# Reordering attention work inside a tuned linear-attention + MLP kernel: kv between transposes, num beside den, and a copy of v on ScalarE

## The chip, the cores and the metric

The kernel runs on one core of a Trainium2 chip. The metric is the device time of one execution in microseconds (us), as a median of several runs; the profile's span is some 1.7 us shorter than the time of the same run (294.94 against 293.2).

## The reference

```python
# q, k, v: (8 batches, 8 heads, 576 positions, 64), float32
def phi(x): return np.where(x > 0, x, np.exp(x) - 1.0) + 1.0
q_p, k_p = phi(q), phi(k)
kv  = einsum('bhsd,bhse->bhde', k_p, v)
z   = sum(k_p, axis=2)
num = einsum('bhsd,bhde->bhse', q_p, kv)
den = einsum('bhsd,bhd->bhs', q_p, z)[..., None] + 1e-06
x   = (num / den), heads side by side: (4608 tokens, 512)
h   = x @ w_in                # 512 -> 2048
out = (h - np.tanh(h)) @ w_out  # 2048 -> 512
```

## The kernel before

The two dense layers run over nine chunks of 512 tokens. Layer 1 makes 16 pieces of hidden features per chunk (4 matmuls each), layer 2 has 16 steps of 4 matmuls. The attention of the later batches is cut into small parts that are hung behind single pieces (`s1[piece]`) or steps (`s2[step]`). In these traces each engine does its work in program order, so the place of a part decides what stands ahead of it on every engine that it uses. In the names, phi, kv, num and den are those of the reference, kz is kv after the mask, and PSUM (`ps_all` in the lines) is the memory, in banks, in which the matmuls' results arrive.

```python
# attention parts (cut)
def a_qT_pe(b, i, banks, on=None):      # 9 TensorE transposes of q's phi, copied out by ScalarE and VectorE
    ...
def a_kv(b, banks):                     # 36 matmuls phi(k)^T v, then the mask product by VectorE -> kz
    ...
def a_vp(b, i):                         # v with its two heads side by side, by VectorE
    nc.vector.tensor_copy(vp[:, i, :, 0:128].rearrange(...), v_b[b % 2][:, 0:2, i])
def a_kv_cols(b, banks):                # the same kv from vp: 36 matmuls, then VectorE's mask products
    ...
    for hg in range(2):
        nc.vector.tensor_mul(kz_t[b][:, hg, :, 0:136], ps[hg], mask[:, hg, :, 0:136])
def a_den(b, banks):                    # 16 small matmuls with kz, then add and reciprocal by VectorE
    ...
def a_spread(b):                        # reciprocals to DRAM (ds) and back, copied to all partitions (rdb)
    ...
def a_num(b, p):                        # one num matmul, then xT = num * rdb by VectorE; two PSUM banks
    ...
# piece pair of layer 1 (cut): tanh by ScalarE, then the subtraction by VectorE
def l1act2(fi, h, gT):
    th = mpool.tile([128, 2, 512], F32, name="th")
    nc.scalar.activation(th, h, AF.Tanh)
    nc.vector.tensor_sub(gT[:, fi:fi + 2, :], h, th)

# chunk 0 (cut)
s2[7].append(lambda: (a_qT_pe(1, 0, side), a_qT_pe(1, 1, side), a_kv(1, side)))
s2[8].append(lambda: b0_scale_rest(side))
s2[9].append(lambda: a_den(1, side))
s2[10].append(lambda: (num1(), a_split(1)))     # num of batch 1: 8 matmuls, five copies (ns) by ScalarE
s2[11].append(lambda: spread1(0))               # reciprocals spread by TensorE, scale by VectorE
# chunk 1 (cut): n1 = 2, n2 = 3
s1[7 if c == 1 else 5].append(lambda: a_kv_cols(n1, attn))
s1[10 if c == 1 else 8].append(lambda: (a_den(n1, attn), a_spread(n1)))
for p in range(NP + 1):
    s2[(11 if c == 1 else 9) + p].append(lambda p=p: a_num(n1, p))
# (cut)
s1[0].append(lambda: (gate(qT_t[n1]), load_k(n2), load_q(n2), load_v(n2)))
#   gate: GpSimd copies one element of q's transpose, so the loads wait for that transfer
```

## Time and profile before

| | before |
|---|---|
| median time | 294.82 us (three runs, 294.65 to 294.93) |
| TensorE busy | 285.2 us of 293.2 (97%) |
| VectorE, ScalarE busy | 60%, 48% |
| gaps of TensorE in the stretch that the change touches | about 2.0 us in all |

The columns of a timeline are: start, length, engine, line, operation, output and inputs, number of instructions merged, and in brackets the idle time of the engine just before with what ended it. A matmul's start is exact, its end is modelled, and starts 0.216 us apart are TensorE's full pace here; so I compare starts. TensorE's lines up to den are shown in the prediction. These are TensorE's later ones, then VectorE's queue ahead of kz (line L202), then the transfers of the reciprocals of batch 2 by SyncE (ds to DRAM, rdb back, here broadcast to all partitions):

```profile
67.30 10.52 PE L387 MATMUL ps_all<-w_out_sb,gT 128*128 128x512 bf16 x48
...
79.85 0.38 PE L317 MATMUL ps_all<-qT,kz 128*128 128x512 bf16 x1
...
58.97 2.34 DVE L373 TENSOR_TENSOR gT<-ps_all,th 128x1024 bf16<-128x1024 f32 x2
61.23 0.78 DVE L202 TENSOR_TENSOR kz<-ps_all,mask 128x272 bf16<-128x272 f32 x2
...
65.45 1.29 SPq L305 DMA_DIRECT2D ds<-rden  x4
70.65 1.12 SPq L308 DMA_DIRECT2D rdb<-ds  x2
```

### The profile page before, as it was taken

To read this page: it belongs to the slowest core of one execution; us is meant where nothing else is said; L and a number is where in the kernel's file an instruction comes from. 1 tells how busy PE (TensorE), PEld (TensorE's weight loads), DVE (VectorE), ACT (ScalarE), POOL (GpSimd) and SP (SyncE) were. 2 spreads that over 40 slices of the span, in tenths; PEclk is the share of its full clock that TensorE was granted. 3 is DMA by queue.
4 is the path that set the end of the run, shared out by engine and by line. 5 is a ranking of instruction groups with operands and counts; after the bars stand their busy time and mean duration, and the time that the engine had idled before them with its cause. 6 is when DMAs were issued, how large, how long until landed. Compare 5 with 4: busy or idle time off the path is not lost.

```text
span 293.2 us, 4504 instructions
## 1 busy us (share of the span) xinstructions
PE 285.2 (97%) x1801; PEld 134.3 (46%) x1801; DVE 174.6 (60%) x265; ACT 139.6 (48%) x168; POOL 33.3 (11%) x55
## 2 busy tenths in 40 slices
PE   8899999999999999999999999999999999999994
PEld 2544453454444444444444445444444444444443
DVE  4759857887567764786478646865581456106600
ACT  4938536947344643455246524661552155126411
POOL 8673030030030003000300020000000000000000
PEclk9999999999999999999999999999999999999999
DMA  6999999998999758955895669667117310131032
GB/s 101 194 204 212 208 207 216 200 145 153 234 163 185 160 118 139 218 117 129 136 223 127 139 134 183 134 154 143 38 24 178 73 36 0 38 84 24 0 74 72
DMA packets 39077, 38.94 MB, mean 133 GB/s; under 512 B 16336, under 2 KB 33808, under 8 KB 38288
## 3 DMA queue, kind: packets, MB, share of 16 engines
q0 software_dynamic: 17552, 18.35, 38.6%
q1 hardware_dynamic: 21344, 20.17, 30.3%
q8 instruction: 14, 0.23, 0.3%
q10 hardware_dynamic: 160, 0.13, 0.1%
q14 instruction: 7, 0.06, 0.1%
HBM read 43.91 MB, written 9.55 MB: 182 GB/s over the span
## 4 chain that ended last, share of the span: by engine, by line
PE 79%; DMA 11%; issue 7%; POOL 2%; DVE 0%; ACT 0%; POOLq 0%
PE ps_all L387 37%; PE ps_all L366 36%; DMA qraw<-in_q_dram 6%; DMA w_in_sb<-in_moe_w_in_dram 3%; PE ps_all L199 2%; DMA kraw<-in_k_dram 2%; PE ps_all L317 2%; PE ps_all L604 1%; PE ps_all L276 1%; POOL qraw L90 0%; ACT e L134 0%; POOL kraw L93 0%; DVE qp L136 0%; POOL v L93 0%; POOL w_out_sb L115 0%
## 5 line engine op out<-in xcount | busy, mean ns | idle before, releaser
L366 PE MATMUL ps_all<-xT,w_in_sb 128*128 128x512 bf16 x576 | 128.0, 379 | 0.3 <-DVE xT L244 0.3
L387 PE MATMUL ps_all<-w_out_sb,gT 128*128 128x512 bf16 x560 | 127.8, 379 | 0.0
L373 DVE TENSOR_TENSOR gT<-ps_all,th 128x1024 bf16<-128x1024 f32 x64 | 77.9, 1218 | 59.8 <-ACT th L372 59.8
L372 ACT ACTIVATE th<-ps_all 128x1024 f32<-128x1024 f32 x64 | 65.5, 1024 | 57.0 <-PE ps_all L366 47.1
L366 PEld LDWEIGHTS <-w_in_sb 128*128 128x128 bf16 x576 | 55.3, 98 | 66.6 <-issue 0.6
L387 PEld LDWEIGHTS <-gT 128*128 128x128 bf16 x560 | 54.1, 98 | 64.3 <-issue 0.3
L396 ACT COPY osb<-ps_all 128x512 f32<-128x512 f32 (+1 forms) x36 | 20.9, 583 | 73.4 <-PE ps_all L387 54.2
L328 DVE TENSOR_TENSOR xT<-ps_all,rdb 128x512 bf16<-128x512 f32 x24 | 16.3, 689 | 13.4 <-PE ps_all L317 11.2
L134 ACT ACTIVATE e<-qraw 128x1152 bf16<-128x1152 bf16 x16 | 18.5, 1162 | 6.9 <-DMA qraw<-in_q_dram 6.9
L134 ACT ACTIVATE e<-kraw 128x1152 bf16<-128x1152 bf16 x15 | 17.5, 1166 | 0.2 <-DMA kraw<-in_k_dram 0.2
L136 DVE TENSOR_TENSOR qp<-e,r 128x1152 bf16<-128x1152 bf16 x16 | 12.0, 757 | 7.8 <-ACT e L134 7.2
L136 DVE TENSOR_TENSOR kp<-e,r 128x1152 bf16<-128x1152 bf16 x15 | 11.4, 759 | 8.3 <-ACT e L134 7.5
L383 POOL COPY g<-qT 1x1 bf16<-1x1 bf16 x5 | 1.2, 240 | 120.6 <-DMA qT<-qp 120.6
L378 DVE TENSOR_TENSOR gT<-ps_all,th 128x512 bf16<-128x512 f32 x16 | 10.3, 685 | 2.4 <-ACT th L377 1.7
L377 ACT ACTIVATE th<-ps_all 128x512 f32<-128x512 f32 x16 | 9.2, 598 | 4.3 <-PE ps_all L366 3.1
L317 PE MATMUL ps_all<-qT,kz 128*128 128x512 bf16 x28 | 10.1, 379 | 0.0
L444 PE MATMUL ps_all<-zero 128*128 128x512 bf16 x29 | 8.8, 463 | 1.2 <-DVE zero L405 1.2
L135 DVE TENSOR_SCALAR r<-qraw 128x1152 bf16<-128x1152 bf16 x16 | 7.3, 453 | 2.2 <-DMA qraw<-in_q_dram 2.2
L199 PE MATMUL ps_all<-vp,kp 64*128 64x136 bf16 x216 | 7.4, 220 | 0.4 <-POOL g L383 0.4
L199 PEld LDWEIGHTS <-kp 64*128 64x128 bf16 x216 | 6.4, 94 | 3.0 <-issue 2.1
L285 DVE RECIPROCAL rden<-den 128x144 f32<-128x144 f32 x7 | 7.4, 1053 | 0.2
L394 DVE COPY osb<-ps_all 128x128 f32<-128x128 f32 x1 | 0.3, 292 | 11.6 <-PE ps_all L604 11.6
(82 smaller groups left out, 121.7 us busy)
## 6 DMA issues: line engine op xcount, KB each, us to landing
out_dram<-osb SPq DMA_DIRECT2D x70, 128.0 KB
rdb<-ds SPq DMA_DIRECT2D x12, 576.0 KB
kraw<-in_k_dram POOLq DMA_DIRECT2D x7, 576.0 KB, 7.1
qraw<-in_q_dram POOLq DMA_DIRECT2D x7, 576.0 KB, 9.0
v<-in_v_dram POOLq DMA_DIRECT2D x7, 576.0 KB, 12.2
w_out_sb<-in_moe_w_out_dram POOLq DMA_DIRECT2D x4, 512.0 KB, 16.4
w_in_sb<-in_moe_w_in_dram POOLq DMA_DIRECT2D x6, 256.0 KB, 8.6
qraw<-in_q_dram POOLq DMA_DIRECT2D x2, 288.0 KB, 4.6
```

The source lines that it names most:

```text
L134: return (lambda: nc.scalar.activation(e, x, AF.Exp), lambda: nc.vector.tensor_scalar(r, x, 0.0, 1.0, ALU.max, ALU.add), lambda: nc.vector ...
L136: lambda: nc.vector.tensor_tensor(y, e, r, ALU.min))
L199: nc.tensor.matmul(ps[hg][:, i, :], kp[r, i, j].rearrange("p h d -> p (h d)"), vp[r, i, j, :], start=(j == 0), stop=(j == J - 1))
L317: nc.tensor.matmul(ps, kz[:, p // 2, p % 2, 0:128], qT[:, p % 2, 0:8, p // 2, :], start=True, stop=True)
L328: nc.vector.tensor_mul(xT[:, p, S * b:S * b + 512].rearrange("p (j t c) -> p j t c", j=8, t=4), ps.rearrange("p j (t c) -> p j t c", t=4), ...
L366: nc.tensor.matmul(h, w_in_sb[:, 2 * (p % 2) + p // 2, fi * 128:(fi + 1) * 128], xT[:, p, c * 512:(c + 1) * 512], start=(n == 0), stop=(n ...
L372: nc.scalar.activation(th, h, AF.Tanh)
L373: nc.vector.tensor_sub(gT[:, fi:fi + 2, :], h, th)
L377: nc.scalar.activation(th, h, AF.Tanh)
L378: nc.vector.tensor_sub(gT[:, fi, :], h, th)
L387: nc.tensor.matmul(o, gT[:, fi, i * 128:(i + 1) * 128], w_out_sb[:, fi, :], start=(fi == 0), stop=(fi == NF - 1))
L396: nc.scalar.copy(osb[:, f0:f1], o[:, f0:f1])
```

## The change

It is meant to fill TensorE's gaps: kv of batch 1 is put between the two sets of transposes, where TensorE waits for VectorE's phi of q; num of batch 1 follows den at once, so that ScalarE has copied it out by the time the spread needs the banks; phi of q of batch 2 moves one step later for it. In layer 1 of chunk 1, one of the two copies of v goes to ScalarE, the second part of phi of k is done later by VectorE, and kv and den of batch 2 move two pieces and one piece later.

```diff
+    def a_vp_act(b, i):
+        nc.scalar.copy(vp[:, i, :, 0:128].rearrange("p j (h d) -> p h j d", h=2), v_b[b % 2][:, 0:2, i])
 ...
-            s2[7].append(lambda: (a_qT_pe(1, 0, side), a_qT_pe(1, 1, side), a_kv(1, side)))
+            s2[7].append(lambda: (a_qT_pe(1, 0, side), a_kv(1, side), a_qT_pe(1, 1, side)))
             s2[8].append(lambda: b0_scale_rest(side))
-            s2[9].append(lambda: a_den(1, side))
-            s2[10].append(lambda: (num1(), a_split(1)))
+            s2[9].append(lambda: (a_den(1, side), num1(), a_split(1)))
             s2[11].append(lambda: spread1(0))
 ...
-            s2[12].append(lambda: q2(0))
-            s2[13].append(lambda: (spread1(1), q2(1)))
-            s2[14].append(lambda: q2(2))
-            s2[15].append(lambda: a_kphi(2, 0))
+            s2[13].append(lambda: (spread1(1), q2(0)))
+            s2[14].append(lambda: q2(1))
+            s2[15].append(lambda: (q2(2), a_kphi(2, 0)))
 ...
-            s1[7 if c == 1 else 5].append(lambda: a_kv_cols(n1, attn))
-            s1[10 if c == 1 else 8].append(lambda: (a_den(n1, attn), a_spread(n1)))
+            s1[9 if c == 1 else 5].append(lambda: a_kv_cols(n1, attn))
+            s1[11 if c == 1 else 8].append(lambda: (a_den(n1, attn), a_spread(n1)))
 ...
-            s1[1].append(lambda: a_kphi(2, 1))
-            for i in range(2):
-                s1[3].append(lambda i=i: a_vp(2, i))
+            k21 = phi_pieces(2, k_t, kp_t, "kp", 1)
+            s1[1].append(k21[0])
+            s1[3].append(lambda: (k21[1](), k21[2](), a_vp(2, 1)))
+            s1[5].append(lambda: a_vp_act(2, 0))
```

## The prediction

> **What bounds the kernel now.** I read the page first, then the list of waits, then the timeline of the stretch that the change touches (layer 2 of chunk 0 and layer 1 of chunk 1), then the landings of transfers.
>
> ```profile
> PE 285.2 (97%) x1801; PEld 134.3 (46%) x1801; DVE 174.6 (60%) x265; ACT 139.6 (48%) x168; POOL 33.3 (11%) x55
> ...
> PE   8899999999999999999999999999999999999994
> ...
> PEclk9999999999999999999999999999999999999999
> ...
> L366 PE MATMUL ps_all<-xT,w_in_sb 128*128 128x512 bf16 x576 | 128.0, 379 | 0.3 <-DVE xT L244 0.3
> L387 PE MATMUL ps_all<-w_out_sb,gT 128*128 128x512 bf16 x560 | 127.8, 379 | 0.0
> ```
> TensorE is busy 97% of the 293.2 us span at full clock. The two dense groups show 379 ns each, but they are pipelined: 64 of them take 13.81 us in the chain, 0.216 us apart. A piece of layer 1 or 2 with 4 matmuls is thus 0.864 us. The change adds and removes no TensorE work, so it can only close TensorE's gaps. Here they are, in the timeline of TensorE:
>
> ```profile
> 37.94 0.68 PE L164 MATMUL ps_all<-ident,qp 128*128 128x128 bf16 x9
> 39.17 0.68 PE L164 MATMUL ps_all<-ident,qp 128*128 128x128 bf16 x9 [0.56 <-DVE qp L136]
> 39.78 1.66 PE L177 MATMUL ps_all<-v,kp 64*128 64x192 bf16 x36
> ...
> 47.26 0.31 PE L354 MATMUL ps_all<-w,sel 32*128 32x144 bf16 x8 [0.69 <-ACT ns L344]
> ...
> 58.74 1.24 PE L199 MATMUL ps_all<-vp,kp 64*128 64x136 bf16 x36 [0.37 <-POOL g L383]
> 59.91 2.76 PE L366 MATMUL ps_all<-xT,w_in_sb 128*128 128x512 bf16 x12
> 62.60 0.43 PE L276 MATMUL ps_all<-qT,kz 128*32 128x144 bf16 x16
> ```
> The columns are start, length, work, and the idle time with its releaser. From start to start the gaps are a little larger, because pipelining hides a piece. The second transposes start 1.23 us after the first where 0.61 is needed (39.17 to 39.78): 0.62 lost. The spread (L354) starts 0.86 us after num and the 4 matmuls of step 11 would have let it (45.54 + 0.864 = 46.40). kv of batch 2 (L199) starts 0.53 after the 32 matmuls before it (51.30 + 6.91 = 58.21). Its releaser is named as POOL, but the copy of v behind it, by VectorE, starts at 58.23 and lasts 0.45; that fits 58.74. Together 2.0 us, which is all there is to win.
>
> **What the Trainium skill says.** *ScalarE: Activation LUTs*, section "What ACT_TABLE_LOAD costs": an ACTIVATE with immediate scale and bias takes 186 ns + 0.833 ns per element, 1146 ns for 1152 elements; the trace has 1162 for exp of that size, so I estimate ScalarE's copy of v at 1.15 us. *VectorE: DVE Perf Modes*, section "Rules for kernel authors": a dense bf16 copy in SBUF runs at 4x; the trace has 450 ns for the same copy on VectorE. So this move pays 1.15 us of ScalarE for 0.41 us of VectorE (two copies take 0.82). *DMA: Bandwidth & Descriptors*, section "Issuing engines are not separate DMA queues": transfers from all engines interleave on the same 16 engines. The trace agrees: 205 to 210 GB/s in every slice from 30 to 40 us while one load of v takes 16.5 us to land.
>
> **The change part by part.**
>
> *kv between the transposes.* It could fill the 0.62 us, since kp is ready at 32.87. But v of batch 1 is not:
>
> ```profile
> 22.28 0.75 POOL L93 DMA_DIRECT2D v<-in_v_dram  x1
> ```
> is the issue of its load in GpSimd's timeline, and the list of DMA issues (last column: us from issue to landing) has for it
> ```profile
> v<-in_v_dram POOLq DMA_DIRECT2D x1, 576.0 KB, 16.5
> ```
> That makes 22.28 + 16.5 = 38.8 us, while kv could start at 37.94 + 0.61 = 38.55. I let kv start at 38.85, end at 40.44 (it took 1.59 to the next matmul), transposes to 41.05. Step 8 then starts at 41.05 in place of 41.37: 0.32 won of 0.62.
>
> *num beside den.* den starts 0.32 earlier too, at 43.00. num follows it at 43.37 and ends at 44.35 (0.98 as now), and steps 10 and 11 bring TensorE to the spread at 46.08. The spread waits for two chains. ScalarE's five copies end 2.64 us after num starts (44.56 to 47.20 now): 46.01. VectorE's split ends 3.22 after den starts (43.32 to 46.54 now): 46.22. So the spread starts at 46.28, not 47.26: 0.98 won, and the releaser turns from ScalarE's ns to VectorE's w. Layer 1 of chunk 1 starts at 50.30 in place of 51.30.
>
> *Layer 1 of chunk 1.* Here ScalarE and VectorE are behind, not TensorE. ScalarE has from the end of step 13 (48.45) no rest: three evictions of 0.47, three exp of 1.07, tanh 0.90, exp 1.07, so the second tanh ends at 56.06. VectorE then runs without a gap: subtraction of pieces 2 and 3 from 56.10 (1.13 from start to start), r and min of k and one copy (0.55 + 0.68 + 0.40), subtractions 4-5, 6-7, 8-9 (3.4), and only then the mask products kz (0.78): they end at 63.0 to 63.1. This is the catch: kv now stands after piece 9 and den after piece 11, so one more subtraction stands in VectorE's queue ahead of kz, between kv and den. TensorE: eight pieces end at 57.21, 0.18 wait for the bank of piece 2, pieces 8 and 9 and kv (1.17) end at 60.29, pieces 10 and 11 at 62.02. den would start there and waits to 63.15 for kz: about 1.1 us lost. kv's own 0.53 wait is gone, since both copies of v are done by 58.9. After den (0.37) piece 12 starts at 63.5; now it starts at 62.97 + 0.86 = 63.83. So of 1.00 + 0.53 won, 0.18 + 1.1 are given back, and 0.3 is left.
>
> *Layer 2 of chunk 1.* There another thing sets the pace:
>
> ```profile
> 79.10 1.89 DVE L328 TENSOR_TENSOR xT<-ps_all,rdb 128x512 bf16<-128x512 f32 x3 [2.26 <-DMA rdb<-ds]
> ```
> VectorE waits 2.26 us for the reciprocals that come back by DMA at 79.10. num has two banks, so its third matmul needs the first product, 79.10 + 0.69 + 0.05 = 79.84; it runs at 79.85. TensorE sits exactly at that limit already, so being 0.3 earlier there buys nothing unless the transfer comes earlier too. Its chain: the reciprocal ends now at 65.42, ds is sent at 65.45, lands with the tail of the loads of k, q and v of batch 3, rdb is sent at 70.65. These loads wait for the gate on the transpose of q (58.27). With the change the reciprocal ends at about 65.8 (kz 63.1, subtraction 63.3 to 64.4, 0.34, 1.05), and the transpose of q is queued behind all eight stores of chunk 0 instead of six, 0.70 us each from 48.2: it is sent at 53.8 in place of 53.48, with less traffic beside it. I estimate rdb between 0.3 earlier and 0.5 later, most likely 0.1 later.
>
> From chunk 2 on nothing changes: TensorE has no gap there (30.35 us per chunk), and VectorE waits for TensorE at L328, not the reverse. **Sum:** the shift at the third num of batch 2, about 0 us: 294.8.
>
> **The rivals.** (1) *The gaps are simply closed*: 0.62 + 0.66 + 0.53 = 1.8 us faster, 293.0. For it: the kernel has 97% of TensorE and these are its last gaps. Against it: v lands at 38.8, and the rdb transfer. (2) *kz late costs more than is won*: if VectorE's queue is 0.5 us later than I add up, the den wait is 1.6 us and rdb comes 0.5 to 1 us later: 295.4 to 295.8. For it: VectorE's queue has no slack from 56 us on. Against it: it has the same durations as before. (3) *The transfer follows the gate*: if the transpose lands earlier, because the stores of chunk 0 no longer run beside it, the loads, ds and rdb come up to 0.4 earlier and the 0.3 survives: 294.5. For it: ds is sent 5 us before rdb, so the loads' end may set it rather than the reciprocal. Against it: the store queue, as computed. (4) *ScalarE's copy of v delays tanh*: the copy ends at about 58.05, tanh of 6-7 starts then, its subtraction only at 59.99: hidden.
>
> **Range and chances.** The start is 294.82, with runs from 294.65 to 294.93. My estimate is 294.8. The low end, 294.1, is the kz wait shorter than I think together with an early transfer; the high end, 295.5, is rival 2. Rival 1 in full lies outside; I give it less than one in ten. Two per cent are 5.9 us, far more than all gaps together and than any wait that I can see: faster 0.01, same 0.98, slower 0.01.
>
> **What would show it.** In the changed profile: kv of batch 1 (L177 now) starts at 38.8 to 38.9, released by the DMA of v; the spread at about 46.3, released by VectorE's w; layer 1 of chunk 1 starts at 50.3; a wait of 0.8 to 1.3 us of den (L276 now) at 62 to 63 us for kz of VectorE; VectorE's L328 again waits for rdb at 79 us, longer than 2.26, and the chain of waits goes through it. Wrong if kv starts at 38.55, if den does not wait for kz, or if rdb lands over 0.5 us from 79.1, which would move the end by the same amount; and if a second gap appears after chunk 2.

## The result

The changed kernel is correct and takes 295.37 us (median of 4 runs, 295.08 to 295.6), against 294.88 for the kernel before in the same rounds. The ratio is 1.0015, with a 95% interval of 0.9998 to 1.0033: the same at the 2% mark.

The timeline of TensorE in the changed kernel (its lines are numbered 3 higher after L189: L390 is layer 2, L369 layer 1, L202 kv of batch 2, L279 den, L320 num, L357 the spread):

```profile
38.03 0.67 PE L164 MATMUL ps_all<-ident,qp 128*128 128x128 bf16 x9
38.76 1.66 PE L177 MATMUL ps_all<-v,kp 64*128 64x192 bf16 x36
40.35 0.68 PE L164 MATMUL ps_all<-ident,qp 128*128 128x128 bf16 x9
41.27 1.02 PE L390 MATMUL ps_all<-w_out_sb,gT 128*128 128x512 bf16 x3 [0.23 <-DMA w_out_sb<-in_moe_w_out_dram]
...
46.49 0.30 PE L357 MATMUL ps_all<-w,sel 32*128 32x144 bf16 x8
...
50.53 8.93 PE L369 MATMUL ps_all<-xT,w_in_sb 128*128 128x512 bf16 x39
59.39 1.24 PE L202 MATMUL ps_all<-vp,kp 64*128 64x136 bf16 x36
60.56 1.90 PE L369 MATMUL ps_all<-xT,w_in_sb 128*128 128x512 bf16 x7
62.96 0.72 PE L279 MATMUL ps_all<-qT,kz 128*32 128x144 bf16 x16 [0.49 <-DVE kz L205]
63.61 3.63 PE L369 MATMUL ps_all<-xT,w_in_sb 128*128 128x512 bf16 x16
67.08 10.52 PE L390 MATMUL ps_all<-w_out_sb,gT 128*128 128x512 bf16 x47
...
79.99 0.38 PE L320 MATMUL ps_all<-qT,kz 128*128 128x512 bf16 x1 [0.23 <-DVE xT L331]
```

The old gaps are gone or small: no 0.56 before the second transposes, 0.20 lost before the spread (44.56 + 8 x 0.216 = 46.29 to 46.49) in place of 0.86, no wait of kv of batch 2. Layer 1 of chunk 1 starts at 50.53, which is 0.77 us earlier than before (51.30). New waits have come: 0.23 for w_out, 0.49 for kz (and more within den, whose 16 matmuls take 0.72 here and 0.43 before), 0.23 at the third num of batch 2. Layer 2 of chunk 1 starts at 67.08, only 0.22 earlier than before (67.30), and the third num at 79.99, 0.14 **later** than before (79.85). VectorE in the same stretch shows the two waits from the other side:

```profile
57.44 0.45 DVE L135 TENSOR_SCALAR r<-kraw 128x1152 bf16<-128x1152 bf16 x1
57.92 0.76 DVE L136 TENSOR_TENSOR kp<-e,r 128x1152 bf16<-128x1152 bf16 x1
58.60 0.45 DVE L189 COPY vp<-v 128x1152 bf16<-128x1152 bf16 x1
58.97 3.59 DVE L376 TENSOR_TENSOR gT<-ps_all,th 128x1024 bf16<-128x1024 f32 x3
62.47 0.78 DVE L205 TENSOR_TENSOR kz<-ps_all,mask 128x272 bf16<-128x272 f32 x2
...
79.24 1.89 DVE L331 TENSOR_TENSOR xT<-ps_all,rdb 128x512 bf16<-128x512 f32 x3 [2.62 <-DMA rdb<-ds]
```

Three subtractions of piece pairs stand in one row ahead of kz; before, it was two. And the first product with the returned reciprocals (rdb) again waits for its transfer, until 79.24. In the queues of GpSimd and SyncE the gate opens at 58.37 (58.29 before), ds is sent 0.66 us later than before, because the reciprocal ends later, and rdb only 0.29 later:

```profile
66.11 1.29 SPq L308 DMA_DIRECT2D ds<-rden  x4
70.94 1.12 SPq L311 DMA_DIRECT2D rdb<-ds  x2
```

From the third num on nothing differs: the span less its start is 293.3 - 79.99 = 213.3 us after and 293.2 - 79.85 = 213.4 before. So the question is what sets the start of the third num. (In both traces no later line of TensorE shows an idle time in brackets.)

### The profile page after: what moved, and what is told of

Same layout as the page of the kernel before. It is cut to its first block, busy times and chain, and to the rows that moved or that the text cites. A ratio compares the mean times of both kernels' runs of the same rounds, so it can differ in the third digit from the quotient of the medians.

```text
span 293.3 us, 4470 instructions
## 1 busy us (share of the span) xinstructions
PE 284.3 (97%) x1772; PEld 134.6 (46%) x1801; DVE 174.5 (60%) x264; ACT 140.5 (48%) x169; POOL 33.2 (11%) x55
## 4 chain that ended last, share of the span: by engine, by line
PE 75%; DMA 18%; POOL 2%; issue 2%; ACT 1%; SPq 1%; DVE 1%; DVEq 0%; POOLq 0%
PE ps_all L369 37%; PE ps_all L390 32%; DMA w_out_sb<-in_moe_w_out_dram 6%; DMA w_in_sb<-in_moe_w_in_dram 3%; DMA rdb<-ds 3%; DMA out_dram<-osb 2%; PE ps_all L202 2%; DMA kraw<-in_k_dram 2%; PE ps_all L320 2%; DMA ds<-rden 1%; PE ps_all L279 1%; POOL v L422 1%; ACT osb L399 1%; SPq L404 0%; POOL qraw L90 0%
## 5 line engine op out<-in xcount | busy, mean ns | idle before, releaser
L369 PE MATMUL ps_all<-xT,w_in_sb 128*128 128x512 bf16 x560 | 127.2, 379 | 1.1 <-DVE xT L247 0.3
L390 PE MATMUL ps_all<-w_out_sb,gT 128*128 128x512 bf16 x547 | 126.1, 379 | 0.9 <-DMA w_out_sb<-in_moe_w_out_dram 0.2
L369 PEld LDWEIGHTS <-w_in_sb 128*128 128x128 bf16 x576 | 55.2, 98 | 66.8 <-issue 0.9
L390 PEld LDWEIGHTS <-gT 128*128 128x128 bf16 x560 | 54.2, 98 | 64.9 <-issue 0.9
L381 DVE TENSOR_TENSOR gT<-ps_all,th 128x512 bf16<-128x512 f32 x16 | 10.3, 685 | 2.4 <-ACT th L380 1.7
L320 PE MATMUL ps_all<-qT,kz 128*128 128x512 bf16 x28 | 10.1, 379 | 0.2 <-DVE xT L331 0.2
L202 PEld LDWEIGHTS <-kp 64*128 64x128 bf16 x216 | 6.4, 94 | 2.5 <-issue 2.1
L202 PE MATMUL ps_all<-vp,kp 64*128 64x136 bf16 x216 | 7.4, 220 | 0.0
```

What stands on the lines that cost most here:

```text
L202: nc.tensor.matmul(ps[hg][:, i, :], kp[r, i, j].rearrange("p h d -> p (h d)"), vp[r, i, j, :], start=(j == 0), stop=(j == J - 1))
L320: nc.tensor.matmul(ps, kz[:, p // 2, p % 2, 0:128], qT[:, p % 2, 0:8, p // 2, :], start=True, stop=True)
L369: nc.tensor.matmul(h, w_in_sb[:, 2 * (p % 2) + p // 2, fi * 128:(fi + 1) * 128], xT[:, p, c * 512:(c + 1) * 512], start=(n == 0), stop=(n ...
L381: nc.vector.tensor_sub(gT[:, fi, :], h, th)
L390: nc.tensor.matmul(o, gT[:, fi, i * 128:(i + 1) * 128], w_out_sb[:, fi, :], start=(fi == 0), stop=(fi == NF - 1))
```

## The experiments

My theory: TensorE's start at the third num of batch 2 is the later of two times, its own arrival and rdb's landing plus 0.75 us (a product of 0.69 that frees the bank, and a hand-over; 79.10 to 79.85 before, 79.24 to 79.99 after). The landing is read as the time at which VectorE's first product starts after waiting for it. What chunk 0 wins is partly lost to VectorE's queue in layer 1 of chunk 1, and the rest to rdb. Rivals: the gaps are simply closed; or the wait for kz alone spoils the change.

First the parts alone. The edits are those of the diff above: `a_kv_only` has the `s2[7]` line alone; `b_num_only` the `s2[9]` to `s2[15]` lines alone; `ab_no_c` both of these, without the edits in chunk 1; `c_l1_only` the edits in chunk 1 alone.

```diff
 # a_kv_only, against before
-            s2[7].append(lambda: (a_qT_pe(1, 0, side), a_qT_pe(1, 1, side), a_kv(1, side)))
+            s2[7].append(lambda: (a_qT_pe(1, 0, side), a_kv(1, side), a_qT_pe(1, 1, side)))
 # b_num_only, against before (q2 one step later as in the change)
-            s2[9].append(lambda: a_den(1, side))
-            s2[10].append(lambda: (num1(), a_split(1)))
+            s2[9].append(lambda: (a_den(1, side), num1(), a_split(1)))
 # ab_no_c, against after
-            s1[9 if c == 1 else 5] ... s1[11 if c == 1 else 8] ... k21 ... a_vp_act(2, 0)
+            s1[7 if c == 1 else 5] ... s1[10 if c == 1 else 8] ... a_kphi(2, 1) ... a_vp(2, i)
 # c_l1_only: the reverse of that, on before
```

> Only kv of batch 1 between its transposes. My theory (transfers set the pace): kv starts at about 38.8 us behind the landing of v, and step 8 of layer 2 in chunk 0 starts at about 41.27, because w_out lands then, so TensorE wins 0.1 us there; spread still released by ScalarE's ns at about 47.15; layer 1 of chunk 1 at about 51.2; third num of batch 2 at 79.8 to 79.9; time within 0.1 us of before. Rival (the gap is simply closed): layer 1 of chunk 1 at 50.7 and the time 0.6 us shorter.

> Only num beside den and the pieces of q moved one step later; kv after both transposes. My theory: spread at about 46.6, released by VectorE's w, layer 1 of chunk 1 at 50.65 (0.65 won), layer 2 of chunk 1 at about 66.7, but the third num of batch 2 waits for rdb and starts at 79.7 to 80.1 as before; time within 0.2 us of before. Rival (nothing binds later): everything after is 0.65 us earlier, third num at 79.2, time 0.65 us shorter.

> The changes in chunk 0 without those in layer 1 of chunk 1. My theory: layer 1 of chunk 1 at 50.5, kv of batch 2 waits for VectorE's copies of v to about 58.0, den of batch 2 does not wait for kz, layer 2 of chunk 1 at about 66.6 (0.7 won), and the third num of batch 2 still waits for rdb, at 79.7 to 80.1: all is lost in that one wait, time within 0.2 us of before. Rival (the later kv and den are what spoils the change): without them the time is 0.7 us shorter than before.

> Only the changes in layer 1 of chunk 1. My theory: den of batch 2 waits about 0.5 to 0.8 us for kz of VectorE, kv no longer waits for a copy of v, layer 2 of chunk 1 starts 0.0 to 0.3 us later than before (67.3 to 67.6), third num of batch 2 at 80.0 to 80.3; time 0.1 to 0.4 us longer than before. Rival (the parts in layer 1 are neutral, and what is lost is lost elsewhere): layer 2 of chunk 1 at 67.3, time equal.

All times below are starts in the timelines of the profiled runs. The first transposes vary from run to run by 0.65 us (37.55 to 38.20 in all these traces; they wait for loads in a saturated stretch), so the last column but three, from the start of layer 1 in chunk 1 to the third num, compares better than the absolute times. Columns two to six are of one traced run each, and in 8 of the 14 kernels and repeats it was the fastest run of its set, while that of the kernel before was not (294.94, against 294.65 to 294.93 in its own set); so a small difference in the traces need not show in the medians, which decide about the time. The median of the kernel before was between 294.87 and 294.99 in all sets of rounds; each ratio is to its own set.

| kernel | layer 1 of chunk 1 | layer 2 of chunk 1 | third num | layer 1 to third num | span | median time | ratio to before (95%) |
|---|---|---|---|---|---|---|---|
| before | 51.30 | 67.30 | 79.85 | 28.55 | 293.2 | 294.88 | |
| after | 50.53 | 67.08 | 79.99 | 29.46 | 293.3 | 295.37 | 1.0015 (0.9998 to 1.0033) |
| a_kv_only | 50.95 | 66.94 | 79.46 | 28.51 | 292.8 | 295.17 | 1.0004 (0.9989 to 1.0019) |
| b_num_only | 50.62 | 66.99 | 79.89 | 29.27 | 293.2 | 294.92 | 1.0000 (0.9985 to 1.0015) |
| ab_no_c | 50.49 | 66.87 | 79.49 | 29.00 | 292.8 | 294.70 | 0.9992 (0.9977 to 1.0007) |
| c_l1_only | 51.15 | 67.32 | 80.25 | 29.10 | 293.6 | 295.44 | 1.0019 (1.0003 to 1.0036) |

**kv alone** wins little, and the reason is in one line. In its timeline, as in the changed kernel's, step 8 of layer 2 waits for weights:

```profile
41.03 1.02 PE L387 MATMUL ps_all<-w_out_sb,gT 128*128 128x512 bf16 x4 [0.25 <-DMA w_out_sb<-in_moe_w_out_dram]
```

From the first transposes to step 8 it takes 41.03 - 37.71 = 3.32 us, against 41.37 - 37.94 = 3.43 before: 0.11 won of the 0.62 lost there. (That w_out sets this start is read from the profile; no run moves that load.) The absolute start of layer 1 at 50.95, earlier than I expected, comes with the run's early first transposes (37.71), and so does the third num at 79.46, 0.3 earlier than expected; the medians show no gain.

**num alone** moves the spread as computed (46.57, layer 1 at 50.62), but kv of batch 2 then waits longer for its copies of v than before (0.74 us instead of 0.37), so layer 2 comes at 66.99, 0.3 later than I expected, and the third num stands at 79.89:

```profile
58.43 1.24 PE L202 MATMUL ps_all<-vp,kp 64*128 64x136 bf16 x36 [0.74 <-DVE vp L189]
...
79.89 0.38 PE L320 MATMUL ps_all<-qT,kz 128*128 128x512 bf16 x1 [0.22 <-DVE xT L331]
```

**Both without chunk 1** has the lowest median of the four, and its rdb came earlier (VectorE takes it at 78.75). I had expected the third num at 79.7 to 80.1 and got 79.49, because rdb came that early. Of the 0.81 us by which layer 1 starts earlier, 0.38 are lost in layer 1 (kv waits 0.75 us in place of 0.37); TensorE would have arrived at 78.52 + 0.864 = 79.38, and only 0.11 are lost to rdb. So "all is lost in that one wait" was wrong.

**Chunk 1 alone** loses: den waits for kz, layer 2 starts 67.32 - 51.15 = 16.17 us after layer 1 (16.00 before), and rdb lands late (79.51). Its reciprocal ends late, so ds is sent at 66.60 instead of 65.45; but v of batch 3 also lands late in this trace (issued at 60.33, landed 11.1 us later, at 71.4; 70.6 before). Which of the two delays rdb is not shown. This run is the only one of the four whose interval excludes 1.

Next, the two suspected limits one at a time and together. rdb is preceded by ds, which is sent at 65.45 in the kernel before but lands only when rdb is sent, at 70.65, with three loads for batch 3 in flight (the last of them, v, is issued at 60.32 and lands 10.3 us later, at 70.6). I held one of them, v, back, by letting GpSimd copy one element that is written later. And I moved kv of batch 2 after piece 8, where its mask products stand ahead of the subtraction of pieces 8 and 9.

```diff
 # before_vlate, after_vlate, after_kv8_vlate
-            s1[0].append(lambda: (gate(qT_t[n1]), load_k(n2), load_q(n2), load_v(n2)))
+            if c == 1:
+                s1[0].append(lambda: (gate(qT_t[n1]), load_k(n2), load_q(n2)))
+            else:
+                s1[0].append(lambda: (gate(qT_t[n1]), load_k(n2), load_q(n2), load_v(n2)))
 ...
+            if c == 1:
+                s2[d + 6].append(lambda: (gate(qp_t[n2]), load_v(n2)))
 # after_kv8, after_kv8_vlate
-            s1[9 if c == 1 else 5].append(lambda: a_kv_cols(n1, attn))
+            s1[8 if c == 1 else 5].append(lambda: a_kv_cols(n1, attn))
```

> The kernel before, with the load of v of batch 3 held back until q of batch 3 has its phi (a one-element copy by GpSimd waits for it). Theory (the transfer of rdb sets the time of the third num of batch 2): ds lands by 69 us, rdb by 77, VectorE no longer waits for it at 79, but TensorE sits at its own limit there (78.95 + 0.864 = 79.81), so the third num starts at 79.8 and the time is that of before within 0.1 us. Rival (rdb does not depend on these loads): rdb still lands at 79.1.

> The changed kernel with v of batch 3 held back in the same way. Theory: no wait of the third num, which starts at 78.73 + 0.864 + 0.05 = 79.6 in place of 79.99; time 0.35 to 0.4 us shorter than the changed kernel, 0.1 to 0.2 shorter than before. Rival (the wait for kz in layer 1 alone sets the end, rdb costs nothing): time as in the changed kernel.

> The changed kernel with kv of batch 2 after piece 8 instead of 9, so that its mask products stand ahead of the subtraction of pieces 8 and 9 in VectorE's queue. Theory: kz ends at about 62.1, den does not wait, layer 2 of chunk 1 starts at about 66.2 (0.9 earlier than in the changed kernel), but rdb still lands at 79.1 to 79.4 and the third num starts at 79.8 to 80.1: no gain in time. Rival (the wait for kz is what spoils the change): time 0.8 us shorter than the changed kernel.

> Both: kv after piece 8, and v of batch 3 held back. Theory: neither wait is left; layer 2 of chunk 1 at about 66.2, rdb by 77.3, third num at about 78.7, the time 1.2 us shorter than the changed kernel and 0.9 to 1.1 shorter than before (293.9). Rival (another limit follows, a third copy of the same pattern): v of batch 3 comes late for its copies at 81 us and takes back part of it, time 294.3 to 294.8.

| kernel | layer 1 of chunk 1 | layer 2 of chunk 1 | third num | layer 1 to third num | span | median time | ratio to before (95%) |
|---|---|---|---|---|---|---|---|
| before_vlate | 51.04 | 67.04 | 79.56 | 28.52 | 293.4 | 295.12 | 1.0008 (0.9995 to 1.0022) |
| after_vlate | 50.18 | 66.72 | 79.24 | 29.06 | 292.9 | 295.11 | 1.0004 (0.9990 to 1.0017) |
| after_kv8 | 50.42 | 66.17 | 80.14 | 29.72 | 293.4 | 295.65 | 1.0026 (1.0011 to 1.0042) |
| after_kv8_vlate | 50.66 | 66.40 | 78.92 | 28.26 | 292.9 | 294.31 | 0.9980 (0.9968 to 0.9993) |

`after_kv8` is the decisive run. den's wait is gone, layer 2 starts 15.75 us after layer 1 (16.55 in the changed kernel, 16.00 before), and TensorE is nearly a microsecond earlier at 66 us. All of it is lost in one wait, in TensorE's and in VectorE's timeline, and the median is even 0.7 us above that of before in its rounds (the interval excludes 1):

```profile
77.61 0.38 PE L320 MATMUL ps_all<-qT,kz 128*128 128x512 bf16 x1
...
80.14 0.38 PE L320 MATMUL ps_all<-qT,kz 128*128 128x512 bf16 x1 [1.30 <-DVE xT L331]
...
79.40 1.89 DVE L331 TENSOR_TENSOR xT<-ps_all,rdb 128x512 bf16<-128x512 f32 x3 [3.69 <-DMA rdb<-ds]
```

With v held back (`after_kv8_vlate`) the same product no longer waits for a transfer, only for its matmul:

```profile
77.18 0.69 DVE L331 TENSOR_TENSOR xT<-ps_all,rdb 128x512 bf16<-128x512 f32 x1 [1.23 <-PE ps_all L320]
```

ds is now sent at 66.29 and rdb at 68.86:

```profile
66.29 1.30 SPq L308 DMA_DIRECT2D ds<-rden  x4
68.86 1.12 SPq L311 DMA_DIRECT2D rdb<-ds  x2
```

That is 2.6 us from one to the other. In the eight traces with all three loads in flight it is 4.4 to 5.5 us, and each of them has rdb sent within 0.6 us of the landing of v, the last load; in the six traces with v held back, rdb is sent 0.1 to 1.0 us after the landing of q, then the last. The interval from layer 1 to the third num, without the limit of rdb, is 28.52 us in `before_vlate`, 29.06 in `after_vlate`, and 28.26 with kv after piece 8. The 0.54 us between the first two are not all due to the edits in chunk 1, since these kernels differ in chunk 0, too. Layer 2 starts 16.00 us after layer 1 before, 16.17 with the edits in chunk 1 alone (`c_l1_only`), 16.38 with those in chunk 0 alone (`ab_no_c`), and 16.55 with both. So the edits in chunk 1 cost 0.17 us, with and without those in chunk 0, and 0.38 are lost because TensorE comes 0.81 us earlier but VectorE's copies of v only 0.43 (57.80 in `ab_no_c` against 58.23 before). From layer 2 to the third num it takes 12.52 us in all traces in which rdb doesn't limit. The changed kernel against the one before is thus, in the traces: -0.77 (layer 1 starts earlier) + 0.55 (layer 1 takes longer) + 0.36 (12.91 against 12.55, the wait for rdb) = +0.14 us.

Not all expectations for these runs were met: `after_vlate` was to be 0.1 to 0.2 us shorter than before and shows no difference (1.0004), and of `after_kv8_vlate` it was the rival that came true. The spans of the kernels with v held back are longer than the third num plus 213.3 us, by 0.5, 0.4 and 0.7 us. The reason is the held-back load: VectorE's copy of v of batch 3 waits for it, with the next subtractions behind it.

```profile
85.65 0.46 DVE L189 COPY vp<-v 128x1152 bf16<-128x1152 bf16 x1 [4.54 <-DMA v<-in_v_dram]
```

So I held v back less, until phi of k of batch 3 is done, 3 to 4 us earlier. The third run of this set takes the ScalarE copy out again.

```diff
 # after_vk, after_kv8_vk, kv8_vk_dve: as ..._vlate, but
-                s2[d + 6].append(lambda: (gate(qp_t[n2]), load_v(n2)))
+                s2[d + 2].append(lambda: (gate(kp_t[n2]), load_v(n2)))
 # kv8_vk_dve, in addition
-            s1[3].append(lambda: (k21[1](), k21[2](), a_vp(2, 1)))
-            s1[5].append(lambda: a_vp_act(2, 0))
+            s1[3].append(lambda: (k21[1](), k21[2](), a_vp(2, 0), a_vp(2, 1)))
```

> The changed kernel, v of batch 3 held back less: until k of batch 3 has its phi (about 73 us), so that it lands by about 80 and VectorE's copies at 81 do not wait for it. Theory (the span is the start of the third num plus 213.3 us when nothing else is late): third num at 79.2 to 79.6, span 292.6 to 292.9, time 0.4 us shorter than the changed kernel; VectorE does not wait for v at 81 us. Rival (the held-back load now delays rdb instead): third num again waits and starts at 79.8 or later.

> kv of batch 2 after piece 8 and v of batch 3 held back until k of batch 3 has its phi. Theory: third num at 78.7 to 78.9 and span = that plus 213.3 = 292.0 to 292.3, against 292.9 with the longer hold; time 293.7 to 294.0, so 0.9 to 1.2 us shorter than before. Rival (the 0.6 us lost with the longer hold have another cause than v's late landing): span 292.9 again.

> The same with both copies of v of batch 2 by VectorE again. What ScalarE's copy is worth: if VectorE's queue is what kv waits for, kv of batch 2 waits about 0.4 us for the first copy and the third num starts 0.3 to 0.4 us later than with ScalarE's copy (79.1 to 79.2), span 292.4 to 292.6. If the copy's engine does not matter: the same start and span as with ScalarE's copy.

| kernel | layer 1 of chunk 1 | layer 2 of chunk 1 | third num | layer 1 to third num | span | median time | ratio to before (95%) |
|---|---|---|---|---|---|---|---|
| after_vk | 50.47 | 67.03 | 79.55 | 29.08 | 292.8 | 294.57 | 0.9985 (0.9972 to 0.9999) |
| after_kv8_vk | 50.23 | 65.98 | 78.50 | 28.27 | 291.8 | 294.08 | 0.9964 (0.9952 to 0.9977) |
| kv8_vk_dve | 50.56 | 66.83 | 79.35 | 28.79 | 292.6 | 294.60 | 0.9989 (0.9974 to 1.0004) |

The copies of v no longer wait (in `after_vk` they run at 81.65 and 82.36), the span is again the third num plus 213.3 us in all three, and `after_vk` needs 29.08 us where `after_vlate` needed 29.06: that interval repeats to 0.02. **`after_kv8_vk` beats the kernel before**: 294.08 us against 294.89, 0.36% less, still "same" at the 2% mark but clear of noise (I had hoped for 293.7 to 294.0); the changed kernel, measured in other rounds, has 295.34 to 295.37.

The last run of the set measures ScalarE's copy of v by itself. Without it kv of batch 2 waits for VectorE, as expected to 0.1 us, and the third num comes 28.79 - 28.27 = 0.52 us later, a little more than the 0.3 to 0.4 expected:

```profile
59.14 1.24 PE L202 MATMUL ps_all<-vp,kp 64*128 64x136 bf16 x36 [0.51 <-DVE vp L189]
```

At last the changed kernel once more, unedited.

> The changed kernel once more, unedited, with more rounds: the first measurement gave 0.5 us more between the medians, but its trace shows only 0.1 us (third num at 79.99 against 79.85). Theory: the third num still starts 0.75 us after rdb lands, the span is that start plus 213.3 us, and a longer run is one whose rdb lands later; ratio to before 1.000 to 1.002. Rival (something outside this chain costs the other 0.4 us): the span is longer than the third num plus 213.3 us by 0.3 or more.

It took 295.34 us (294.93 to 296.02), before 294.87 in the same rounds, ratio 1.0021 (1.0008 to 1.0035): a small loss, of 0.2 to 1.0 us. Its trace repeats the first one: layer 1 to the third num in 29.53 us, third num at 79.89, span 293.2, so it shows no loss in absolute time. But this trace, like the first, is of the fastest of the kernel's runs (294.93 and 295.08), so it can't show where the typical run's other 0.4 us lie; and set against the trace of the kernel before, which is of a typical run (294.94), it makes the loss look smaller than it is. A hint is in the times: holding v back in the changed kernel (`after_vk`) moves the third num by 0.38 us between the traced runs (29.46 to 29.08), but the median by 0.8 us, and its four runs lie within 0.2 us (294.47 to 294.67), against 0.5 and 1.1 us for the changed kernel's. That would fit an rdb that lands later in most runs than in the traced ones. Against it: with v held back, `after_vlate` still spreads over 0.86 us (294.71 to 295.57), and `after_kv8_vk` has a median 0.5 us above its traced run. No trace of such a run is at hand; this stays open.

## Why the prediction was right, step by step

The range held (294.1 to 295.5; measured 295.37 and 295.34), and the class, "within 2%", was right. The point, 294.8, was 0.5 us low. That the range held is in part luck: its upper end stood for rival 2 (den waits 1.6 us, rdb lands 0.5 to 1 us later), and the measured time lies near that end without either having happened in the trace (0.95 and 0.14).

- **kv between the transposes would wait for v and win only 0.32 us.** Half right. kv started at 38.76 (predicted 38.85), and five of the later runs name v's DMA as its releaser. But I missed the next transfer of the same issuer, GpSimd: w_out for step 8 lands 17.8 us after its issue at 23.43, just before 41.27. The term of 0.32 was 0.10, and layer 1 of chunk 1 came at 50.53, not 50.30.
- **The spread is released by w, 5.23 us after step 8.** Right: 46.49 - 41.27 = 5.22; w ends at 46.43, just before the spread, ScalarE's last copy already at 46.22.
- **VectorE's queue makes den wait about 1.1 us for kz.** Right. TensorE is through pieces 10 and 11 at 60.56 + 8 x 0.216 = 62.29, resumes layer 1 at 63.61, and den alone takes 0.37: 0.95 lost. `after_kv8` takes this wait away with one edit, and `c_l1_only` shows it alone (0.71 lost). It was 0.15 shorter than predicted, and chunk 0's gain 0.2 smaller, so that the two errors nearly cancel: layer 2 of chunk 1 came 0.22 us earlier than before, where I had 0.3.
- **The third num stands at rdb's limit, so what is left buys nothing.** Right, and it is the step that carries the result. I had rdb most likely 0.1 later; it was 0.14 later, and the third num with it. In `after_kv8` TensorE comes most of a microsecond earlier and gets none of it; with v held back it gets it.
- **Why rdb is late.** My rival 3 (rdb follows the loads' end) had the right mechanism: holding one load back lets ds land in 2.3 to 3.4 us (six traces) in place of 4.4 to 5.5 (eight). Its size did not occur, since the transpose was not sent earlier (53.57 against 53.48). Whether the reciprocal's end matters as well stays open: in `c_l1_only` ds is sent 1.15 us later than before and rdb lands 0.4 later, though the gate opens no later (58.13), but v lands 0.8 later there, too.
- **Rival 1 (the gaps are closed, 293.0)** failed, as it was given; even the best version reaches 294.08.
- **ScalarE's copy of v.** The estimate of 1.15 us, from the Trainium skill, *ScalarE: Activation LUTs*, section "What ACT_TABLE_LOAD costs" (1146 ns from its formula), was good to 3%: the trace has 1.18 us. As in the answer to rival 4, it stays hidden: the subtractions run on without a gap from 58.97.
- **The 16 DMA engines are shared.** The slice given as agreement (30 to 40 us) holds loads of GpSimd alone, so it can't show that transfers of several issuers interleave. What bears on it is SyncE's ds, which takes 4.4 to 5.5 us beside three of GpSimd's loads and 2.3 to 3.4 beside two.
- **The sum "about 0 us".** The traced runs agree (+0.1 us), though the one of the changed kernel is its fastest; the medians say +0.5. The rest of the loss is measured, not explained.

## What to carry to other kernels

When the busiest engine is at 97%, a closed gap counts only as far as the next thing that comes at a fixed time: look for the later waits that already stand at zero slack, above all transfers, and work out what they will do if the engine arrives earlier. Moving a part later in program order also puts more of the other engines' work ahead of it; here one subtraction of 1.1 us ahead of the mask products cost more (29.06 - 28.26 = 0.80 us) than the copy moved to ScalarE won (0.52 us, measured with kv after piece 8). In this kernel it also paid to keep a load that was not needed yet out of the way of a tiny transfer whose result was needed soon.

## What the Trainium skill lacked or had wrong

- *DMA: Bandwidth & Descriptors*, section "Queues, rings and completion order", says that each engine takes turns between queues packet by packet, and the section "Anatomy of one DMA — SWDGE (gpsimd) path" has about 2.0 us of fixed cost for a transfer issued by GpSimd. The page has no figure for a small transfer beside bulk loads on another queue: ds (4 transfers of 4.5 KB, issued by SyncE) took from its first issue until rdb could be sent 5.2 us beside three loads (65.45 to 70.65), 2.3 us where only the tail of a load was left and the core's 16 DMA engines were 14% busy (94.11 to 96.40 in the next chunk), and 2.3 to 3.4 us with one of the three loads held back.
- *DMA: Bandwidth & Descriptors*, section "Bandwidth", has no entry for loads that convert float32 to bf16, as this kernel's do. With its 16 engines saturated (30 to 40 us) the kernel before showed 206 to 210 GB/s in the profile's count, and one 576 KB load took 16.5 us to land in the crowd.
